# Evacuating the first two gates and values for 384 tokens early, with a transfer moved ahead and a set of copies moved later, in a fused attention and SwiGLU kernel

## Chip, cores and metric

One core of a Trainium2 chip. The metric is device time in microseconds (us), the median of several executions; the record puts all runs quoted in the fast state. Engines: PE is TensorE (matmul), PEld its weight loads, DVE is VectorE, ACT is ScalarE, POOL is GpSimd, which here issues the DMAs of the inputs and weights.

## The reference

```python
# q, k, v: (8, 8, 576, 64) = batch, head, token, dim; window 128, ALiBi slopes
scores = scale * q @ k.T                 # scale = 1/8
mask = (rel >= 0) & (rel < 128)          # rel = query position - key position
attn = softmax(where(mask, scores - slope[h] * |rel|, -1e9))
x = (attn @ v), heads joined             # (4608, 512)
g = x @ w_gate                           # (512, 1536)
out = (g * sigmoid(g) * (x @ w_val)) @ w_out     # (4608, 512) float32
```

## The kernel before

The attention works in tiles ("units") of 128 tokens; the feed-forward part works in blocks n of 512 tokens, that is four units, and in 12 column blocks m of 128. PE does every matrix product and, early on, the transposes; it writes them to PSUM, where each gate or value product fills one bank. While attention is still producing tokens, gate and value products of finished blocks fill PE. A gate is `tt` = tanh of half the product on ACT, `uu` = (tt + 1) times the product on DVE; a value product is multiplied into `hT` on DVE.

The first four units are put in order by hand. The gate and value products of m = 0, 1, 2 of block 0 are begun there for the units that are ready (`begin`), and finished when the fourth unit has been transposed:

```python
    def wide(n, m, which, c1=512):          # the product, columns c0..c1 of one PSUM bank
        ...
        for kb in range(NKB):
            nc.tensor.matmul(ps[:, c0:c1], w[:, kb, ms], xT[n][:, kb, c0:c1],
                             start=(kb == 0 and c0 == 0), stop=(kb == NKB - 1 and c1 == 512))
        if c1 < 512:
            early[(n, m, which)] = (ps, c1)
        return ps

    def gate_val(n, m):
        if n not in hT:
            hT[n] = hpool.tile([P, NMB, 512], FP16, name="hT", tag="hT")
        pg = wide(n, m, "g")
        tt = supool.tile([P, 512], FP16, name="tt", tag="tt")
        nc.scalar.activation(tt, pg, AF.Tanh, scale=0.5)
        uu = supool.tile([P, 512], FP16, name="uu", tag="uu")
        nc.vector.scalar_tensor_tensor(out=uu, in0=tt, scalar=..., in1=pg,
                                       op0=ALU.add, op1=ALU.mult)
        yield
        pv = wide(n, m, "v")
        nc.vector.tensor_mul(hT[n][:, m, :], uu, pv)
        yield

    def first_tiles():
        ...
        begin(6, 2)
        begin(4, 3)                 # g and v of m = 0, 1 for 384 tokens
        x_transposed(FIRST - 1)     # the fourth unit
        begin(6, 3)
```

The first eight steps of the feed-forward part are still in program order; after that the framework's scheduler chooses the order on PE, DVE and ACT from the dependencies:

```python
        with tc.manual_schedule(engines=ENGINES[MANUAL]):   # PE, DVE, ACT in program order
            first_tiles()
            done = FIRST
            steps = progress(ffn())
            while (at := next(steps)) < ALONE:              # ALONE = 8
                if at == 2.0:
                    nc.scalar.copy(idm2, idm)
                if at == 5.0:
                    make_masks()                            # 4 copies on ACT
        for step in steps:                                  # from here the scheduler orders
            ...
```

The loads stand in one queue:

```python
    load(4)
    load_qk(5, "q")
    load_w(512, 1024)        # W slices: 512 KB of w_gate, then 512 KB of w_val
    load_qk(5, "k")
    load_v(5)
    load_w(1024, 1536)
    load(6)                  # k6, q6, v6
    load(7)
    load(8)
    ...                      # then wo, the output weights, in two halves
```

## Time and profile before

| | before |
|---|---|
| time, median of 3 runs | 357.24 us (357.01 to 357.49) |
| PE busy in the profiled execution | 341.5 of 355.1 us |
| PE idle, 25 to 55 us | 2.71 us |
| largest PE waits there | 1.15 us (DVE), 0.81 us (q of unit 6 landing) |

PE is the bound, so a gain can only be a PE wait that goes away and is not given back later. The lines are in the prediction below. In timelines the columns are start (us), length (us), engine, source line, operation, output<-inputs, shapes, type, count; in brackets the engine's idle time just before and what ended it. "pg" and "pv" are gate and value products, "pt" transposed q or k, "ps" and "psc" scores, "px" a transposed x, "po" the output projection.

### The profile page before, as it was taken

How to read it: one execution, taken by the hardware profiler on the slowest of the kernel's cores; microseconds unless marked ns; L12 is line 12 of the kernel's file. 1: busy time of each engine (PE TensorE's matmuls, PEld its weight loads, DVE VectorE, ACT ScalarE, POOL GpSimd, SP SyncE). 2: the span in 40 equal slices, each digit the busy share in tenths (PEclk: the TensorE clock that was granted, in tenths of full speed). 3: DMA queues.
4: the chain of work that ended last, by engine and by line, in shares of the span. 5: the costliest groups of instructions: out<-in, count | busy, mean ns of one | idle time of the engine just before them, and what ended most of it. 6: DMA issues, size and time to landing. Idle time of an engine off the chain costs nothing.

```text
span 355.1 us, 7251 instructions
## 1 busy us (share of the span) xinstructions
PE 341.5 (96%) x2765; PEld 196.8 (55%) x2765; DVE 273.1 (77%) x595; ACT 178.2 (50%) x353; POOL 106.9 (30%) x132
## 2 busy tenths in 40 slices
PE   7898999999999999999999999999999999999995
PEld 4683454544456655565456655564666566456643
DVE  4858786997977799678986998799878965975540
ACT  4847584555555454555555555455444323332321
POOL 8964755544838354543500100000000000000000
PEclk9999999999999999999999999999999999999999
DMA  9999999999999999999995413311022101101114
GB/s 150 171 186 188 136 184 153 92 149 129 154 134 178 155 147 170 169 144 166 181 73 105 66 55 30 90 31 59 17 75 55 50 2 59 62 0 62 39 43 96
DMA packets 157763, 37.34 MB, mean 105 GB/s; under 512 B 147232, under 2 KB 153248, under 8 KB 157728
## 3 DMA queue, kind: packets, MB, share of 16 engines
q0 software_dynamic: 116224, 18.62, 84.3%
q1 hardware_dynamic: 41056, 17.97, 27.5%
q8 instruction: 21, 0.34, 0.4%
q10 hardware_dynamic: 448, 0.30, 0.3%
q14 instruction: 14, 0.11, 0.1%
HBM read 37.91 MB, written 9.44 MB: 133 GB/s over the span
## 4 chain that ended last, share of the span: by engine, by line
PE 71%; DVE 11%; DMA 6%; ACT 5%; POOL 4%; issue 3%; DVEq 0%; ACTq 0%; POOLq 0%
PE pg L368 21%; PE pv L368 21%; PE po L477 14%; PE av L319 4%; DMA qn<-in_q_dram 4%; PE po L398 3%; PE ps L254 3%; DVE uu L381 2%; DVE hT L385 2%; PE p L477 2%; DMA wv_sb<-in_moe_w_val_dram 2%; ACT ex L259 2%; PE px L345 2%; DVE ex L263 2%; ACT exc L286 1%
## 5 line engine op out<-in xcount | busy, mean ns | idle before, releaser
L368 PE MATMUL pg<-xT,wg_sb 128*128 128x512 f16 (+2 forms) x464 | 116.4, 365 | 0.3 <-ACT xT L346 0.2
L368 PE MATMUL pv<-xT,wv_sb 128*128 128x512 f16 (+2 forms) x464 | 114.7, 365 | 1.6 <-DVE uu L381 1.6
L379 ACT ACTIVATE tt<-pg 128x512 f16<-128x512 f32 x108 | 65.1, 604 | 85.7 <-PE pg L368 82.3
L381 DVE SCALAR_TENSOR_TENSOR uu<-tt,pg 128x512 f16<-128x512 f16 x107 | 73.0, 683 | 38.1 <-ACT tt L379 37.7
L385 DVE TENSOR_TENSOR hT<-uu,pv 128x512 f16<-128x512 f16 x108 | 73.7, 682 | 6.1 <-PE pv L368 2.3
L368 PEld LDWEIGHTS <-wv_sb 128*128 128x128 f16 x464 | 42.7, 98 | 38.8 <-issue 3.1
L368 PEld LDWEIGHTS <-wg_sb 128*128 128x128 f16 x464 | 42.4, 98 | 35.1 <-issue 2.9
L259 ACT ACTIVATE ex<-ps 128x512 f16<-128x512 f32 x96 | 50.1, 605 | 9.8 <-PE ps L254 9.8
L168 POOL DMA_DIRECT2D va<-in_v_dram x40 | 34.1, 856 | 50.3 <-PE av L319 36.0
L174 POOL DMA_DIRECT2D qn<-in_q_dram x39 | 33.6, 864 | 27.9 <-DMA qT<-qn 19.6
L174 POOL DMA_DIRECT2D kn<-in_k_dram x39 | 33.2, 860 | 25.6 <-DMA kT<-kn 15.7
L477 PEld LDWEIGHTS <-hT 128*128 128x128 f16 x336 | 31.8, 98 | 15.4 <-issue 3.5
L263 DVE TENSOR_TENSOR ex<-ex,m_reg 128x1024 f16<-128x1024 f16 x48 | 32.5, 686 | 8.3 <-ACT ex L259 8.3
L477 PEld LDWEIGHTS <-S 128*128 128x128 f16 x252 | 23.9, 98 | 11.7 <-issue 2.9
L322 DVE TENSOR_TENSOR x<-av,rec 128x256 f16<-128x256 f32 x72 | 28.9, 419 | 0.6
L477 PE MATMUL po<-T,S 128*128 128x256 f16 x168 | 23.0, 273 | 0.6 <-ACT p5s L495 0.6
L477 PE MATMUL po<-T,hT 128*128 128x256 f16 x168 | 23.1, 272 | 0.4
L286 ACT ACTIVATE exc<-psc 128x512 f16<-128x512 f32 x40 | 21.4, 608 | 3.4 <-PE psc L282 3.4
L346 ACT COPY xT<-px 128x512 f16<-128x512 f16 x24 | 14.1, 586 | 15.3 <-PE px L345 15.3
L319 PEld LDWEIGHTS <-ex 128*128 128x128 f16 x384 | 18.4, 97 | 4.9 <-issue 0.7
L319 PE MATMUL av<-va,ex 128*128 128x65 f16 x384 | 20.4, 193 | 0.5
L398 PE MATMUL po<-wo_sb,hT 128*128 128x512 f16 x84 | 19.7, 379 | 0.0
(74 smaller groups left out, 289.7 us busy)
## 6 DMA issues: line engine op xcount, KB each, us to landing
out_dram<-osb SPq DMA_DIRECT2D x32, 256.0 KB, 2.5
va<-in_v_dram POOLq DMA_DIRECT2D x32, 128.0 KB, 8.6
qn<-in_q_dram POOLq DMA_DIRECT2D x31, 128.0 KB, 8.7
kn<-in_k_dram POOLq DMA_DIRECT2D x31, 128.0 KB, 8.1
wo_sb<-in_moe_w_out_dram POOLq DMA_DIRECT2D x2, 768.0 KB, 9.4
wg_sb<-in_moe_w_gate_dram POOLq DMA_DIRECT2D x2, 512.0 KB, 10.7
wv_sb<-in_moe_w_val_dram POOLq DMA_DIRECT2D x2, 512.0 KB, 11.8
out_dram<-osb SPq DMA_DIRECT2D x6, 128.0 KB, 2.4
```

What stands on the lines that cost most here:

```text
L168: nc.gpsimd.dma_start(va[rank][p0:p1, :, 0:D], src)
L174: nc.gpsimd.dma_start(t_[p0:p1], src)
L259: nc.scalar.activation(e[:, o:o + 2, :], banks[q4][par], AF.Exp, scale=scale)
L263: nc.vector.tensor_mul(e[:, o, :], e[:, o, :], reg[:, o, :])
L319: nc.tensor.matmul(av[:, j, :], w, val, start=(n == 0), stop=(n == len(todo) - 1))
L322: nc.vector.tensor_mul(x[:, 4 * half:4 * half + 4, :], av[:, :, 0:D], rec.broadcast_to([P, 4, D]))
L368: nc.tensor.matmul(ps[:, c0:c1], w[:, kb, ms], xT[n][:, kb, c0:c1], start=(kb == 0 and c0 == 0), stop=(kb == NKB - 1 and c1 == 512))
L379: nc.scalar.activation(tt, pg, AF.Tanh, scale=0.5)
L381: nc.vector.scalar_tensor_tensor(out=uu, in0=tt, scalar=one if (n, m) == PIN else 1.0, in1=pg, op0=ALU.add, op1=ALU.mult)
L385: nc.vector.tensor_mul(hT[n][:, m, :], uu, pv)
L398: nc.tensor.matmul(po, hT[n][:, m, j * P:(j + 1) * P], wo_sb[:, m, :], start=(i == 0), stop=(i == NMB - 1))
L477: nc.tensor.matmul(dst, a[:, m, cols], b[:, m, :], start=(start and m == 0), stop=(m == HM - 1), skip_group_check=True)
```

## The change

Its intent: let ACT and DVE work off three quarters of the first two gates and values while the fourth unit is still on its way (DVE is idle there), so that DVE comes sooner to the `uu` that PE waits for; load k and q of unit 6 before v5 and the last W slices, so that PE need not wait for q6; and move the mask copies out of ACT's way to step 18.

```diff
--- before.py
+++ after.py
@@ -18,6 +18,7 @@
 WIN = 128
 QK_DMA_FROM = 11
 X_DMA_FROM = 24
+MASKS_AT = 18.0
 ALONE = 8
 MANUAL = "compute"
 ET = mybir.EngineType
@@ -366,23 +367,34 @@
             ps = pool.tile([P, 512], FP32, name="p" + which, tag=tag)
         for kb in range(NKB):
             nc.tensor.matmul(ps[:, c0:c1], w[:, kb, ms], xT[n][:, kb, c0:c1],
-                             start=(kb == 0 and c0 == 0), stop=(kb == NKB - 1 and c1 == 512))
+                             start=(kb == 0 and c0 == 0), stop=(kb == NKB - 1 and c1 == 512),
+                             skip_group_check=(n == 0))
         if c1 < 512:
             early[(n, m, which)] = (ps, c1)
         return ps
 
-    def gate_val(n, m):
+    acted = {}
+
+    def gate(n, m, pg, c0=0, c1=512):
+
+        if (n, m) not in acted:
+            acted[(n, m)] = [supool.tile([P, 512], FP16, name=i, tag=i) for i in ("tt", "uu")]
+        tt, uu = (t_[:, c0:c1] for t_ in acted[(n, m)])
+        nc.scalar.activation(tt, pg[:, c0:c1], AF.Tanh, scale=0.5)
+        nc.vector.scalar_tensor_tensor(out=uu, in0=tt, scalar=one if (n, m) == PIN else 1.0,
+                                       in1=pg[:, c0:c1], op0=ALU.add, op1=ALU.mult)
+
+    def val(n, m, pv, c0=0, c1=512):
+
         if n not in hT:
             hT[n] = hpool.tile([P, NMB, 512], FP16, name="hT", tag="hT")
-        pg = wide(n, m, "g")
-        tt = supool.tile([P, 512], FP16, name="tt", tag="tt")
-        nc.scalar.activation(tt, pg, AF.Tanh, scale=0.5)
-        uu = supool.tile([P, 512], FP16, name="uu", tag="uu")
-        nc.vector.scalar_tensor_tensor(out=uu, in0=tt, scalar=one if (n, m) == PIN else 1.0, in1=pg,
-                                       op0=ALU.add, op1=ALU.mult)
-        yield
-        pv = wide(n, m, "v")
-        nc.vector.tensor_mul(hT[n][:, m, :], uu, pv)
+        nc.vector.tensor_mul(hT[n][:, m, c0:c1], acted[(n, m)][1][:, c0:c1], pv[:, c0:c1])
+
+    def gate_val(n, m):
+        c0 = 384 if (n, m) in acted else 0
+        gate(n, m, wide(n, m, "g"), c0)
+        yield
+        val(n, m, wide(n, m, "v"), c0)
         yield
 
     def rows_of(n, j):
@@ -594,7 +606,11 @@
                 x_transposed(i - 1)
         begin(6, 2)
         begin(4, 3)
+        gate(0, 0, early[(0, 0, "g")][0], 0, 384)
         x_transposed(FIRST - 1)
+        val(0, 0, early[(0, 0, "v")][0], 0, 384)
+        gate(0, 1, early[(0, 1, "g")][0], 0, 384)
+        val(0, 1, early[(0, 1, "v")][0], 0, 384)
         begin(6, 3)
 
     def attention():
@@ -636,9 +652,10 @@
     load_qk(5, "q")
     load_w(512, 1024)
     load_qk(5, "k")
+    load_qk(6)
     load_v(5)
     load_w(1024, 1536)
-    load(6)
+    load_v(6)
     load(7)
     load(8)
     loaded = 9
@@ -675,9 +692,9 @@
             while (at := next(steps)) < ALONE:
                 if at == 2.0:
                     nc.scalar.copy(idm2, idm)
-                if at == 5.0:
-                    make_masks()
         for step in steps:
+            if step == MASKS_AT:
+                make_masks()
 
             b1 = 24 + 3 * PRE
```

`skip_group_check` only turns off a check in the framework; the refactoring into `gate` and `val` issues the same instructions where nothing is split.

> **What bounds the kernel now.** I read the page first, then the windows (busy time of each engine in chosen stretches), then the instruction timeline of the stretch the change touches, then the chain that ended last.
>
> ```profile
> PE 341.5 (96%) x2765; PEld 196.8 (55%) x2765; DVE 273.1 (77%) x595; ACT 178.2 (50%) x353; POOL 106.9 (30%) x132
> DMA  9999999999999999999995413311022101101114
> ```
>
> TensorE (PE) is busy 341.5 of 355.1 us, so at most 13.6 us can be gained by closing gaps anywhere; the DMA engines are full up to slice 22, so in the part I look at a transfer lands when its turn comes. The windows say where the gaps are. Columns: stretch, its length, busy time of PE, PEld, DVE, ACT, POOL, then clock, DMA share, GB/s.
>
> ```profile
> 20.00:30.00 10.00, 8.41 (x112) 6.59 (x109) 5.75 (x13) 6.24 (x13) 5.86 (x7) 1.00 1.72 186
> 30.00:35.00 5.00, 5.00 (x28) 2.10 (x27) 3.98 (x7) 3.04 (x6) 2.46 (x4) 1.00 1.42 197
> 35.00:40.00 5.00, 4.01 (x30) 1.89 (x29) 3.31 (x6) 2.39 (x5) 3.20 (x5) 1.00 2.46 154
> 40.00:45.00 5.00, 5.00 (x42) 2.55 (x42) 4.79 (x11) 3.62 (x7) 4.26 (x6) 1.00 1.59 128
> 45.00:50.00 5.00, 4.84 (x59) 2.61 (x57) 4.55 (x11) 4.36 (x10) 3.74 (x5) 1.00 1.21 192
> 50.00:55.00 5.00, 4.80 (x69) 2.85 (x69) 4.28 (x12) 4.49 (x10) 2.10 (x3) 1.00 2.02 167
> 200.00:250.00 50.00, 49.76 (x387) 28.27 (x386) 44.83 (x101) 25.44 (x51) 0.88 (x1) 1.00 0.22 53
> ```
>
> From about 40 us on PE is at 96 to 100%, so what PE saves before 40 us should reach the end, unless something before about 60 us gives it back. Between 20 and 40 us PE stands still for 1.59 + 0.99 = 2.6 us. The timeline names those gaps (in brackets: idle time before, and who ended it):
>
> ```profile
> 24.16 0.38 PE L368 MATMUL pg<-xT,wg_sb 128*128 128x128 f16 x4 [0.23 <-ACT xT L346]
> 27.34 0.38 PE L201 MATMUL pt<-idm,qn 128*128 128x128 f16 x4 [0.21 <-DVE uu L381]
> 28.87 1.04 PE L368 MATMUL pv<-xT,wv_sb 128*128 128x512 f16 x4 [1.15 <-DVE uu L381]
> 35.28 1.02 PE L368 MATMUL pv<-xT,wv_sb 128*128 128x512 f16 x4 [0.18 <-DVE uu L381]
> 37.34 0.40 PE L201 MATMUL pt<-idm,qn 128*128 128x128 f16 x4 [0.81 <-DMA qn<-in_q_dram]
> ```
>
> 0.23 + 0.21 + 1.15 + 0.18 + 0.81 = 2.58 us: all of it. The gap at 28.87 is the value of column block m=3, which needs the PSUM buffer that uu of m=2 reads out of. DVE comes to that one late:
>
> ```profile
> 25.21 0.69 DVE L381 SCALAR_TENSOR_TENSOR uu<-tt,pg 128x512 f16<-128x512 f16 x1 [4.07 <-ACT tt L379]
> 26.01 0.69 DVE L385 TENSOR_TENSOR hT<-uu,pv 128x512 f16<-128x512 f16 x1
> 26.23 0.63 ACT L109 COPY m_c<-m_reg 128x512 f16<-128x512 f16 x1
> 28.14 0.68 DVE L381 SCALAR_TENSOR_TENSOR uu<-tt,pg 128x512 f16<-128x512 f16 x1
> 28.53 0.60 ACT L379 ACTIVATE tt<-pg 128x512 f16<-128x512 f32 x1
> ```
>
> DVE was idle 4.07 us waiting for the first tanh, then had two full gate/value pairs to do before the uu that PE wanted; and the four mask copies (26.23 to 28.50 on ACT) held the fourth tanh until 28.53. The gap at 37.34 is tile 6's q, which the chain of waits follows back to its issue:
>
> ```profile
> 24.32 12.98 DMA qn<-in_q_dram
> 37.34 0.40 PE pt L201 x4
> ```
>
> **What the Trainium skill says.** (1) "PSUM — Partial Sum Buffer", section "PSUM bank collisions raise a hardware error": two engines may not touch one bank in the same quadrant at once, whatever the columns, so same-bank accesses of different engines are ordered by dependencies. That is the change's hidden cost: DVE reads columns 0 to 384 of a bank into which PE must still write 384 to 512. The trace before agrees: X and Y in the second product are two halves of one bank, and PE's next product into X waits for ACT's read of Y.
>
> ```profile
> 120.49 0.41 ACT L495 ACTIVATE p5s<-po 128x256 f32<-128x256 f32 x1
> 120.95 0.82 PE L477 MATMUL po<-T,S 128*128 128x256 f16 x6 [0.31 <-ACT p5s L495]
> ```
>
> (2) "ScalarE: Activation LUTs", section "What ACT_TABLE_LOAD costs": an activation with immediate scale and bias takes 186 ns + 0.833 ns per column, 613 ns for 512; the trace has 604. So splitting one in two costs one fixed part. (3) "DMA: Bandwidth & Descriptors", section "Two DMAs through the same engine are not ordered": within one queue of one engine descriptors start in order. So q of tile 6 lands behind everything issued before it; the trace agrees in size: 12.98 us to landing with two W slices ahead, 8.7 us for the median q load.
>
> **The change, part by part.** *Split gates.* Durations: tanh 604 ns for 512 columns and 290 ns for the 128-column copy of the identity on ACT, so 0.82 ns a column: 384 columns about 500 ns, 128 about 290. DVE 683 ns for 512 and 419 for 256 (row L322), so 1.03 ns a column: 550 and 290. A gate/value pair on DVE repeats every 1.40 us now (25.21 to 26.61); scaled by columns, 1.14 us for 384 and 0.61 for 128. Two more tanh and four more DVE operations cost about 0.4 us of ACT and 0.6 us of DVE in all, most of it in idle time.
>
> Laid on the trace: pg of m=0 for three tiles is ready at 22.6, tanh to 23.1 (before the xT copy at 23.52, so that copy is not delayed), uu to 23.7, hT to 24.35. The tanh of m=1 must follow the xT copy (its end 24.11): to 24.6, uu to 25.2, hT to 25.85. Now the bank rule: PE's last-tile matmuls for pg0 are free at 24.16 as today, pv0 at 24.4, but pg1 waits for uu (25.2, today 24.60) and pv1 for hT (25.9, today 24.83). So PE runs 1.05 us later here: pg2, pv2, pg3 follow to 27.4, then the three transposes (today at 26.36, 26.75, 27.34; 0.22 each) to 28.1. DVE meanwhile does the four 128-column remainders, 25.85 to 27.1, then uu of m=2 at 27.15 to 27.83 instead of 28.14 to 28.82. So pv3 starts at about 28.1 instead of 28.87: **gain 0.8 us**, not the whole 1.36, because about one microsecond of wait moves to pg1 and pv1.
>
> *Tile 6 ahead of the last W slices.* q6 jumps two W slices of 512 KB and v5 of 128 KB. At the 186 GB/s of the window 20 to 30 that is 1.15 MB / 186 = 6.2 us, so it lands at about 31 instead of 37.3. The wait of 0.81 goes, and the wait that the 0.8 us of the first part would only have lengthened does not form: **gain 0.8 us**. The W slices land later by k6 and q6, 256 KB, 1.4 us: wv landed just before 35.70 (a POOL load waited for it until then), so 37.1. Its first use is the value of m=8, at 41.07 today and about 39.4 after: still in time by 2 us.
>
> *Masks.* 2.46 us of ACT leave 26 to 28.5, where after the split the fourth tanh is wanted at 27.6; they come back after step 18, about 40 us. There ACT is busy 3.62 + 4.36 + 4.49 = 12.47 of 15 us; with 2.46 more it is 14.9 of 15. Exp, kT and xT copies queue behind the masks. PE has other matmuls to put between, and ACT is slack from 55 us (57.09 follows 1.77 us of idleness), so I charge **0.5 us**, chosen between 0 and 1.
>
> The 0.18 at 35.28 may go or stay: 0.1. wo lands at about 52.5 and is first used at 54.62; PE arrives up to 1.7 us earlier, still just behind. Sum: 0.8 + 0.8 + 0.1 - 0.5 = 1.2 us; 357.24 - 1.2 = 356.0. I shade it to **355.8**, since the fixed mask time may be hidden entirely.
>
> **The rivals.** *A, the bank wait takes it all:* if ACT starts the first tanh after the xT copy, everything of the split slides 0.6 to 1 us and PE waits on DVE in new places for as long as it does now. For it: PE is in program order here. Against: 0.4 us of margin between 23.1 and 23.52. Time: 356.3 with the load order still gaining, 357 with the mask cost. *B, ACT becomes the bound from 40 to 55 us:* 14.9 of 15 us busy; PSUM buffers come free late and PE gains holes of 1 to 2 us. Time: 357 to 357.8. *C, all 2.6 us of gaps close and the masks are free:* 354.7. *D, reshuffling:* after the first eight steps the framework's scheduler orders the instructions, and any earlier change can give another order of transposes, scores and gates over 300 us; PE's idle time there is 13.6 - 2.6 - about 4 at the start, 7 us, so I give it +-0.8 either way.
>
> **Range and chances.** The best case is near 354.5 (C with some luck of D), the poor case near 357.3 (B). Range 354.4 to 357.2. Faster by over 2% would need 7.1 us, almost three times all gaps in the stretch: 0.01. Slower by over 2%: nothing moved is that large, 0.005. Within 2%: 0.985.
>
> **What would show it right or wrong.** Right: uu and hT on 384 columns between 23 and 26 us, DVE's idle 4.07 us cut to about 2; new short PE waits "<-DVE uu" or "<-DVE hT" before the 128-column pg/pv of m=1, around 1 us in sum; pv3 near 28.1; no DMA wait before q6's transpose; PE idle in 20 to 40 us down from 2.6 to about 1.1; ACT near 100% in a stretch after 40 us with mask copies in it. Wrong: no waits at pg1 and pv1 (then bank order cost nothing and the gain is nearer 2 us); wv's last slice awaited by PE at m=8; PE holes in 40 to 55 us larger than 1 us with ACT as releaser; or a different total from gaps after 60 us, which none of my steps covers except D.

## The result

| | before | after |
|---|---|---|
| median | 357.24 us (3 runs) | 356.09 us (4 runs, 356.04 to 356.26) |
| ratio, 95% interval | | 0.9969 (0.9951 to 0.9986) |
| PE idle, 25 to 55 us | 2.71 us | 1.94 us |
| marker (below) | 32.73 us | 31.73 us |

Ratios here and below are the mean time of one kernel's fast runs over that of the other's of the same rounds, so not quite the ratio of the medians quoted. (The record of the result lists a fourth run of the kernel before, equal to the median.) The time fell by 1.15 us, which is within 2%, and inside the predicted range, 0.3 us above the predicted 355.8.

Where it came from is read in the windows of the kernel after (columns as in the prediction):

```profile
20.00:30.00 10.00, 9.12 (x117) 7.14 (x113) 6.53 (x17) 4.92 (x12) 5.80 (x8) 1.00 1.82 181
30.00:35.00 5.00, 4.72 (x32) 2.17 (x30) 3.91 (x8) 3.25 (x7) 3.27 (x6) 1.00 1.44 200
35.00:40.00 5.00, 5.00 (x42) 2.64 (x41) 4.58 (x9) 3.80 (x8) 2.59 (x4) 1.00 2.19 163
50.00:55.00 5.00, 4.26 (x54) 2.47 (x53) 4.67 (x12) 4.01 (x8) 1.75 (x2) 1.00 1.95 166
```

The first PE number is the one to follow. In 20 to 40 us PE is idle 0.88 + 0.28 + 0 = 1.16 us, where it was 2.58: the predicted 1.1. But in 50 to 55 us it is idle 0.74 us, where it was 0.20: something was given back. The PE timeline of the kernel after has both, the repaired places and the new waits:

```profile
25.34 0.38 PE L369 MATMUL pg<-xT,wg_sb 128*128 128x128 f16 x4 [0.33 <-DVE uu L384]
26.00 0.38 PE L369 MATMUL pv<-xT,wv_sb 128*128 128x128 f16 x4 [0.28 <-DVE hT L391]
...
27.75 0.22 PE L202 MATMUL pt<-idm,qn 128*128 128x128 f16 x1
28.02 1.02 PE L369 MATMUL pv<-xT,wv_sb 128*128 128x512 f16 x4
...
29.74 0.55 PE L202 MATMUL pt<-idm,qn 128*128 128x128 f16 x7
...
31.88 0.61 PE L255 MATMUL ps<-qT,kT 64*128 64x256 f16 x8
...
34.75 1.02 PE L369 MATMUL pv<-xT,wv_sb 128*128 128x512 f16 x4 [0.21 <-DVE uu L384]
...
35.83 0.39 PE L202 MATMUL pt<-idm,qn 128*128 128x128 f16 x4
...
44.00 0.61 PE L255 MATMUL ps<-qT,kT 64*128 64x256 f16 x8
...
51.32 0.29 PE L346 MATMUL px<-idm,x 128*128 128x128 f16 x2 [0.23 <-DVE x L323]
...
52.25 0.28 PE L346 MATMUL px<-idm,x 128*128 128x128 f16 x2 [0.32 <-DVE x L323]
...
56.09 0.81 PE L410 MATMUL po<-wo_sb,hT 128*128 128x512 f16 x3
```

The bank waits are there (0.33 and 0.28), pv of m = 3 starts at 28.02 without a wait, and q6 is transposed at 35.83 without one. The wait of 0.21 us for `uu` at 34.75 stayed, and two new waits for `x` of the attention stand at 51.32 and 52.25. The last lines answer to these of the kernel before, its PE timeline:

```profile
29.84 0.28 PE L254 MATMUL ps<-qT,kT 64*128 64x256 f16 x2
...
44.81 0.62 PE L254 MATMUL ps<-qT,kT 64*128 64x256 f16 x8
...
56.89 0.81 PE L398 MATMUL po<-wo_sb,hT 128*128 128x512 f16 x3
```

The first scores after the hand-ordered part start at 29.84 before and at 31.88 after, which is taken up with the experiments. The scores that start at 44.81 start 0.81 us earlier after the change, and the last three matmuls of the first output projection, at 56.89, start 0.80 us earlier.

On DVE the idle 4.07 us ahead of the first `uu` are halved, and its 384 columns take the predicted 0.55 us (DVE timeline of the kernel after):

```profile
23.36 0.55 DVE L384 SCALAR_TENSOR_TENSOR uu<-tt,pg 128x384 f16<-128x384 f16 x1 [2.00 <-ACT tt L383]
```

The mask copies, moved to step 18 in the text, were to appear on ACT after 40 us. ACT's timeline has the first of them here:

```profile
7.04 0.62 ACT L110 COPY m_c<-m_reg 128x512 f16<-128x512 f16 x1
```

All four run from 7.04 to 9.31 us, right after the exponentials that make their source. The scheduler, free to place them, put them *earlier*, into time when ACT had been idle waiting for the first scores (2.14 us before the change, 0.20 now). "Later" in the program was 19 us earlier on the chip.

**A marker.** The start of a run jitters: the last-unit matmuls of pg0 start at 24.16 in the profiled execution of the kernel before, at 24.36 after, and between 23.8 and 24.8 in the experiments, in no relation to their edits. Absolute times of different traces therefore carry some 0.5 us of noise. (PE's wait for q6 in the kernels with the old load order is the exception: it ends between 37.32 and 37.67 in all five traces.) I take as marker the time from those matmuls (the line at 24.16 in the prediction) to the last three matmuls of the first output projection (56.89 and 56.09): 56.89 - 24.16 = 32.73 before, 56.09 - 24.36 = 31.73 after. It fell by 1.0 us, the time by 1.15. In all fourteen traces the stretch from the first to the last of these holds the same 276 matmuls, kind by kind, so that the marker compares equal work in different orders. After about 57 us PE's idle time agrees between the kernels, stretch by stretch (0.27 us in 60 to 80, 0.46 in 80 to 100, 0.98 in 150 to 200, 0.24 in 200 to 250), so nearly all of the difference arises inside the marker.

### The profile page after: what moved, and what is told of

It is laid out like the page before. It is cut to its first block, busy times and chain, and to the rows that moved or that the text cites. A ratio compares the mean times of both kernels' runs of the same rounds, so it can differ in the third digit from the quotient of the medians.

```text
span 354.5 us, 7261 instructions
## 1 busy us (share of the span) xinstructions
PE 341.5 (96%) x2765; PEld 197.5 (56%) x2765; DVE 273.4 (77%) x599; ACT 178.9 (50%) x355; POOL 106.9 (30%) x132
## 2 busy tenths in 40 slices
DMA packets 157763, 37.34 MB, mean 105 GB/s; under 512 B 147232, under 2 KB 153248, under 8 KB 157728
## 4 chain that ended last, share of the span: by engine, by line
PE 73%; DVE 16%; ACT 7%; issue 3%; DVEq 0%; ACTq 0%
PE pv L369 20%; PE pg L369 20%; PE po L489 14%; PE av L320 4%; DVE uu L384 4%; DVE hT L391 3%; PE ps L255 3%; PE po L410 3%; DVE ex L264 3%; PE p L489 2%; ACT ex L260 2%; PE px L346 2%; ACT tt L383 2%; ACT exc L287 2%; DVE x L323 1%
## 5 line engine op out<-in xcount | busy, mean ns | idle before, releaser
L383 ACT ACTIVATE tt<-pg 128x512 f16<-128x512 f32 (+2 forms) x110 | 65.5, 596 | 85.2 <-PE pg L369 81.8
L384 DVE SCALAR_TENSOR_TENSOR uu<-tt,pg 128x512 f16<-128x512 f16 (+2 forms) x109 | 73.4, 674 | 34.6 <-ACT tt L383 33.9
L391 DVE TENSOR_TENSOR hT<-uu,pv 128x512 f16<-128x512 f16 (+2 forms) x110 | 74.0, 673 | 7.1 <-PE pv L369 2.2
L347 ACT COPY xT<-px 128x512 f16<-128x512 f16 x24 | 14.1, 586 | 14.9 <-PE px L346 14.8
```

The lines of the kernel that those rows point to most:

```text
L383: nc.scalar.activation(tt, pg[:, c0:c1], AF.Tanh, scale=0.5)
L384: nc.vector.scalar_tensor_tensor(out=uu, in0=tt, scalar=one if (n, m) == PIN else 1.0, in1=pg[:, c0:c1], op0=ALU.add, op1=ALU.mult)
L391: nc.vector.tensor_mul(hT[n][:, m, c0:c1], acted[(n, m)][1][:, c0:c1], pv[:, c0:c1])
```

## The experiments

**Theory.** The load order gives the whole gain. The split does locally what was worked out, but alters the order that the scheduler gives PE afterwards, and what it wins is lost through that order. **Rivals:** (1) the bank waits take the split's gain; (2) each part gives its predicted share (0.8, 0.8, -0.5); (3) the masks cost time where they are.

The experiments ran in three groups of four, each with its own runs of the kernel before beside it (medians 357.06 to 357.20), each group on another chip (7, 10 and 2 in the record), so that kernels of different groups are compared by their ratios to before. All had 5 rounds, and all gave the right result. PE idle is over 25 to 55 us of the profiled execution; it is a coarser measure than the marker, as its edges don't move with the jitter.

| kernel | median us (range) | ratio to before (95%) | marker | PE idle |
|---|---|---|---|---|
| before | 357.24 | 1 | 32.73 | 2.71 |
| the change | 356.09 | 0.9969 (0.9951 to 0.9986) | 31.73 | 1.94 |
| e_split_only | 358.27 (358.19 to 358.45) | 1.0033 (1.0020 to 1.0045) | 33.90 | 3.71 |
| e_load_only | 355.92 (355.61 to 356.30) | 0.9968 (0.9955 to 0.9980) | 31.75 | 1.90 |
| e_masks_only | 356.99 (356.78 to 357.18) | 0.9996 (0.9983 to 1.0010) | 32.38 | 2.35 |
| e_load_masks | 356.18 (355.96 to 356.43) | 0.9973 (0.9961 to 0.9986) | 31.75 | 1.90 |
| e_split_load | 357.06 (356.86 to 358.78) | 1.0003 (0.9988 to 1.0018) | 32.79 | 2.82 |
| e_split_masks | 357.78 (357.68 to 358.05) | 1.0017 (1.0005 to 1.0029) | 33.11 | 3.12 |
| e_masks_late | 355.85 (355.80 to 356.29) | 0.9963 (0.9951 to 0.9976) | 31.70 | 1.83 |
| e_fill | 354.94 (354.77 to 356.16) | 0.9942 (0.9930 to 0.9954) | 30.43 | 0.85 |
| e_qk_first | 355.81 (354.84 to 357.82) | 0.9963 (0.9941 to 0.9986) | 30.55 | 1.00 |
| e_one_early | 355.27 (354.91 to 357.69) | 0.9961 (0.9939 to 0.9984) | 30.59 | 1.10 |
| e_fill_masks_old | 355.69 (354.85 to 358.13) | 0.9964 (0.9940 to 0.9988) | 32.07 | 2.43 |
| e_fill_old_load | 358.61 (356.84 to 358.91) | 1.0025 (1.0007 to 1.0043) | 34.00 | 2.61 |

### The three parts, alone

**Only the split.** The load order and the place of the masks are those of before:

```diff
--- the change
+++ e_split_only
-    load_qk(6)
     load_v(5)
     load_w(1024, 1536)
-    load_v(6)
+    load(6)
@@
                     nc.scalar.copy(idm2, idm)
+                if at == 5.0:
+                    make_masks()
         for step in steps:
-            if step == MASKS_AT:
-                make_masks()
```

> The kernel before with the split gates alone (old load order, masks still made at step 5). Theory A (the parts hang on one another): q of tile 6 lands near 37.3 us whatever PE does before it, so all that the split wins by 28 us is lost again in a longer wait before q6's transpose: wait there 0.8 -> about 1.3 to 1.6 us, total 357.0 to 357.3, same as before. Rival B (the parts add up): the split gives 0.5 us or more by itself, total at or below 356.7, wait at q6 no longer.

Measured: 358.27 us, slower than before, ratio 1.0033 with an interval above 1; marker 33.90, 1.2 us longer. That is 1 us above even the 357.0 to 357.3 expected. PE's timeline:

```profile
30.70 1.02 PE L369 MATMUL pv<-xT,wv_sb 128*128 128x512 f16 x4 [0.51 <-DVE uu L384]
...
37.35 0.40 PE L202 MATMUL pt<-idm,qn 128*128 128x128 f16 x4 [1.24 <-DMA qn<-in_q_dram]
...
53.71 0.28 PE L346 MATMUL px<-idm,x 128*128 128x128 f16 x2 [0.66 <-DVE x L323]
```

Two things are to be seen. The wait for q6 has grown from 0.81 to 1.24 us and ends at 37.35, as it did before (37.34): the landing does not move with PE, and what PE wins ahead of it is spent waiting at it. All of the loss therefore comes after it, where there are waits for the attention's `x` (0.66 us at 53.71) that the kernel before did not have. Rival 2 does not hold: the split alone is worth less than nothing.

**Only the load order.** The split's four calls are taken out and the masks are at step 5 again:

```diff
--- before
+++ e_load_only
+    load_qk(6)
     load_v(5)
     load_w(1024, 1536)
-    load(6)
+    load_v(6)
```

> The kernel before with the load order alone. Theory A: q6 lands near 31 us, the 0.81 us wait before its transpose goes, the 1.15 us gap at 28.87 stays; PE ahead by 0.8 us at 40 us and, since the stretch up to 57 us gives nothing back as long as no more than about 0.8 is won, total 356.4 to 356.6. Rival C (the attention chain from 42 to 54 us sets the time whatever is won before it): no change, 357.1 to 357.3.

Measured: 355.92 us, ratio 0.9968, marker 31.75. The change as a whole has 0.9969 and 31.73. PE's timeline:

```profile
28.56 1.04 PE L369 MATMUL pv<-xT,wv_sb 128*128 128x512 f16 x4 [1.15 <-DVE uu L384]
...
36.05 0.39 PE L202 MATMUL pt<-idm,qn 128*128 128x128 f16 x4
```

The wait of 1.15 us for `uu` is untouched, the wait for q6 is gone. It is faster than either reading expected. Two lines of edit give as much as the whole change.

**Only the masks.**

```diff
--- before
+++ e_masks_only
                     nc.scalar.copy(idm2, idm)
-                if at == 5.0:
-                    make_masks()
         for step in steps:
+            if step == MASKS_AT:
+                make_masks()
```

> The kernel before with the masks alone moved to step 18. The built order puts the four mask copies right after the eight exponentials of the first masks, near 7 us, not later: ACT waits there for the first scores anyway. Theory A: fourth tanh comes earlier, but PE then waits the longer for q6 (37.3): 357.0 to 357.3. Rival B (parts add): 0.2 to 0.4 us gained, 356.9. A third reading: the copies at 7 us delay the first exp by 0.2 us (the kernel after starts its first exp 0.2 us later than before), then 357.4; if the first exp starts at 9.3 with the masks in front, that 0.2 was chance.

Measured: 356.99 us, ratio 0.9996 (0.9983 to 1.0010): no difference that the runs can tell. The marker is 0.35 us shorter only because this trace starts 0.33 us late (24.49) while the wait for q6 ends where it did (37.32): where PE waits for a landing, the jitter of the start enters the marker.

### The three parts, in pairs

**Without the split:** the change with these four lines taken out.

```diff
--- the change
+++ e_load_masks
-        gate(0, 0, early[(0, 0, "g")][0], 0, 384)
         x_transposed(FIRST - 1)
-        val(0, 0, early[(0, 0, "v")][0], 0, 384)
-        gate(0, 1, early[(0, 1, "g")][0], 0, 384)
-        val(0, 1, early[(0, 1, "v")][0], 0, 384)
         begin(6, 3)
```

> The change without the split gates (load order and masks). Theory A: the 1.15 us gap at 28.87 stays near 1 us since it hangs on DVE's order, the q6 wait goes; total 356.3 to 356.6, so the split's share on top is 0.2 to 0.5 us. Rival C: what is won before 42 us beyond about 0.8 us is taken back by the attention chain, so this is already as fast as the whole change, 356.1.

Measured: 356.18 us, ratio 0.9973, marker 31.75. Its interval and that of the change overlap almost wholly: **inside the change the split is worth nothing that the runs can tell**, where 0.8 us had been predicted.

**Without moving the masks:** the change with `make_masks()` back at step 5 (the mask lines of the first diff above).

> The change without the move of the masks (made at step 5, on ACT near 26 to 29 us). Theory A with free masks: the mask copies hold the fourth tanh back to about 28.5 us and the uu of m=3 to about 29.5; PE has other work, so 0 to 0.3 us slower than the change: 356.1 to 356.4. If the masks were the larger part of what was won: 356.7 or more.

Measured: 357.06 us, ratio 1.0003 (five of six runs 356.86 to 357.23, one 358.78), marker 32.79. The split and the load order together, with masks in their old place, gain nothing. `make_masks` at step 5 puts 2.3 us of copies on ACT just before the tanh of m = 3; PE then waits at 30.81 for the `uu` that follows:

```profile
30.81 1.02 PE L369 MATMUL pv<-xT,wv_sb 128*128 128x512 f16 x4 [0.51 <-DVE uu L384]
```

In the trace DVE itself had been idle 1.31 us for that tanh. After this wait PE's order is another one than in the change. So beside the split the old place of the masks costs about 1 us; how much of it is this wait and how much the order, these runs don't separate. Rival 3 is partly right: the masks matter, but only together with the split.

**Without the load order:** the change with `load(6)` behind the W slices again (the load lines of the first diff above).

> The change without the load order. Theory A: PE is at q6's transpose about 1.5 us early and waits about 1.5 to 2.2 us for it; total 357.0 to 357.3, the same as before. Rival B: 356.5, as the split keeps its own share.

Measured: 357.78 us, ratio 1.0017, marker 33.11. PE waits 1.21 us for q6, to 37.63. This is slower than before, by more than the expectation had it (357.0 to 357.3), and the wait is shorter than the 1.5 us or more expected. Beside the change (0.9969) the load order is worth 0.0048, 1.7 us: more than alone. Without it the wait there is 0.4 us longer than before (1.21 against 0.81).

### Where the split's gain went

**Masks really late.** As the scheduler had hoisted the copies, the cost that I had charged them had not been tried. Here they are held behind the tanh of m = 8:

```diff
--- the change
+++ e_masks_late
+    tanhs = []
@@
-        nc.scalar.activation(tt, pg[:, c0:c1], AF.Tanh, scale=0.5)
+        tanhs.append(nc.scalar.activation(tt, pg[:, c0:c1], AF.Tanh, scale=0.5))
@@
             if step == MASKS_AT:
-                make_masks()
+                with tc.issue_after(tanhs[-1].ins):
+                    make_masks()
```

> The change with the four mask copies forced behind the tanh of m=8 on ACT (near 40 us), which is what the prediction took the change to do. The prediction's step: ACT then close to full from 40 to 55 us and 0.5 us (0 to 1) lost against the change: 356.6. Rival: PE has enough other work, or the scheduler orders around it: 356.1, no difference.

Measured: 355.85 us, ratio 0.9963, marker 31.70: no slower than with the masks at 7 us. The copies start at 40.22 in its trace. The predicted cost of 0.5 us does not come even where the copies are as late as I had assumed.

**The bank waits filled.** The change finishes m = 1 before it takes up m = 2. Here PE does the last-unit matmuls of m = 2, whose banks nobody is reading, before those of m = 1, while DVE reads the banks of m = 1:

```diff
--- the change
+++ e_fill
+    whole = {}
@@
-        gate(n, m, wide(n, m, "g"), c0)
+        gate(n, m, whole.pop((n, m, "g"), None) or wide(n, m, "g"), c0)
         yield
-        val(n, m, wide(n, m, "v"), c0)
+        val(n, m, whole.pop((n, m, "v"), None) or wide(n, m, "v"), c0)
+        if (n, m) == (0, 0):
+            for which in "gv":
+                whole[(0, 2, which)] = wide(0, 2, which)
         yield
```

> The change with the last-tile matmuls of m=2 issued on PE before those of m=1, so that PE has 0.45 us of work while DVE still reads the two banks of m=1. Theory: the waits of 0.33 and 0.28 us before pg1 and pv1 come from the reads of the first 384 columns in the same bank; they shrink by about 0.45 us in sum. In the total: 355.7 if what is won there reaches the end; 356.1 (no change) if, as theory C has it, the attention chain between 42 and 54 us takes back whatever is won before it.

Measured: 354.94 us, ratio 0.9942 (0.9930 to 0.9954), marker 30.43. It beats both kernels, and its interval just does not meet that of e_load_only (on another chip): here the split does gain, and more than the 355.7 expected at best. The marker is 1.3 us shorter than the change's, though, and the bank waits had only 0.33 + 0.28 = 0.61 us to give (one of them, 0.28, remains). The rest must come from elsewhere. The order on PE shows what: in the kernel before PE does the transposes k4, q4, q5 (12 matmuls) and then pv of m = 3. In the change it does k4, one matmul of q4 (27.75 in the fence of the result), pv of m = 3, the next gate, and only then the other seven (29.74). So the scores that need q5 (keys of unit 4, queries of units 4 and 5; the recorded expectation below calls them those of unit 5) start 7.5 us after the marker's start instead of 5.7. In e_fill the order is the old one, and those scores start at 5.7 again. Filling the waits and the order are mixed in this experiment; the next takes them apart.

**The order restored, the bank waits kept.** The transposes of unit 4 are put into the hand-ordered part, ahead of pv of m = 3; nothing else changes:

```diff
--- the change
+++ e_qk_first
                     nc.scalar.copy(idm2, idm)
+                if at == 7.0:
+                    transposes_to(need[FIRST])
         for step in steps:
```

> The change with the transposes of k4, q4 and q5 put by hand before pv3 (in the kernel after, the scheduler does only one of q4's, then pv3 and pg4, then the other seven, so that the first scores of unit 5 start 7.5 us after the last-tile pg0 instead of 5.7 as before; from there on all of PE's order differs from before). The bank waits before pg1 and pv1 stay (0.6 us). Theory D (the split earns nothing in the change because of that other order): from the transposes on the order is that of before, scores at about 6 us, the lead of PE kept up to the end of block 0, total 355.2 to 355.7. Rival (the bank waits themselves eat the gain): 356.0 to 356.2 as the change.

Measured: median 355.81 us, ratio 0.9963, in neither of the two ranges expected. The profiled execution took 354.98 us, with marker 30.55 and PE idle 1.00 us. The timeline of PE:

```profile
25.35 0.38 PE L369 MATMUL pg<-xT,wg_sb 128*128 128x128 f16 x4 [0.33 <-DVE uu L384]
26.01 0.38 PE L369 MATMUL pv<-xT,wv_sb 128*128 128x128 f16 x4 [0.28 <-DVE hT L391]
...
27.76 0.61 PE L202 MATMUL pt<-idm,qn 128*128 128x128 f16 x8
...
30.08 0.61 PE L255 MATMUL ps<-qT,kT 64*128 64x256 f16 x8
...
54.92 0.81 PE L410 MATMUL po<-wo_sb,hT 128*128 128x512 f16 x3
```

All eight matmuls of q4 and q5 stand together, and the scores follow at 30.08. The bank waits are still 0.33 and 0.28 us, the same as in the change, and yet the marker is 1.2 us shorter than the change's (31.73) and than that of e_load_only (31.75). **Rival 1 falls:** the bank waits do not take the split's gain. The order did: with it kept, the split is worth 31.75 - 30.55 = 1.2 us in the marker, somewhat more than predicted. Why the scheduler chose the other order, no run shows.

How an order costs PE time is read from the traces and not tested by itself. The matmuls are the same. Gates that PE takes before the scores are gates that it no longer has to put into the pauses of the attention chain (scores, exp, multiplication, weighted values, x), and those pauses then show as waits for `x`: 0.23 us at 51.32 and 0.32 at 52.25 in the change; neither e_load_only nor e_qk_first has them (each is idle 0.20 us in 50 to 55, the change 0.74). The times of this kernel have two values, three of six near 355.0, the others 356.3 to 357.8, so its ratio of 0.9963 does not separate it from the change; the argument rests on the markers, one trace of each kernel, and the 1.2 us is what the better half of the runs shows. More on this below.

**Only the first gate and value early.**

```diff
--- the change
+++ e_one_early
         val(0, 0, early[(0, 0, "v")][0], 0, 384)
-        gate(0, 1, early[(0, 1, "g")][0], 0, 384)
-        val(0, 1, early[(0, 1, "v")][0], 0, 384)
         begin(6, 3)
```

> The change with only the first gate and value evacuated early, not the second: no wait before pg1 and pv1, DVE has one full pair (1.40 us) and one 128-column pair (0.61) to do before the uu of m=2; the built order is like before after the transposes. If the early second gate is worth its bank waits: 355.7 to 356.0; if the first gate alone brings it: 355.0 to 355.4, near the fill version's 354.95.

Measured: 355.27 us, ratio 0.9961, marker 30.59. The bank waits are gone, and pv of m = 3 waits 0.61 us for `uu` instead: as much as the two together (0.61). The order is the good one. So the second early gate and value only move a wait from one place to another, and half of the split does as well as all of it. With the new load order, the four kernels with a split and the old order of transposes have markers of 30.43 to 30.59 (after a wait for `wo` in one of them, below, is taken off), the three with the other order 31.70 to 32.79: the order goes with the gain in all seven.

### What comes next on the path

**Filled, with the masks in the old place:** e_fill with `make_masks()` at step 5.

> The fill version with the masks back at step 5 (26 to 29 us on ACT); its PE order is the same as the fill version's, so this is the cost of the masks by themselves. Theory: the fourth tanh waits for the four copies (about 2 us later), PE waits 0.5 us for a uu: 355.4 to 355.6 against 354.95. Rival (masks only mattered through the order they caused, 1.1 us between the change and the change without the move): no difference, 354.9 to 355.1.

Measured: 355.69 us, ratio 0.9964; three of its six runs lie at 354.9 to 355.2, the others above 356. Up to the output projection, 28.1 us after the marker's start, PE's timeline is that of e_fill to within 0.1 us, but for one matmul that changes sides of the first scores, and the wait of 0.5 us expected for `uu` is not there: with that order of PE, the old place of the masks costs nothing. But the profiled execution (356.19 us) has a wait that e_fill's (354.82 us) has not, here at PE and at POOL:

```profile
53.92 1.89 PE L414 MATMUL po<-wo_sb,hT 128*128 128x512 f16 x8 [1.64 <-DVE x L323]
```

```profile
54.16 1.75 POOL L169 DMA_DIRECT2D va<-in_v_dram  x2 [4.59 <-DMA wo_sb<-in_moe_w_out_dram]
```

The profile names DVE's `x`, but DVE had long finished it; POOL's next load, which waited for `wo`, the output weights, until 54.16, shows what landed then. Without the 1.64 us the marker is 32.07 - 1.64 = 30.43, e_fill's to the digit. POOL's wait for `wo` ends between 52.27 and 53.37 in the other thirteen traces, and e_fill starts the projection at 52.50. So in the kernels that are fast up to there PE arrives just when the second half of `wo` lands, and a late landing costs it a wait. In this run that accounts for the 1.4 us beside e_fill's; that the other runs above 356 us wait there too is likely, but no profile caught one. The runs at 357.7 to 358.1 in this group (and the 358.78 of e_split_load) remain unexplained, but the record has a hint: their mean granted clock is 0.994 or 0.995, while no other run of the kernels named so far is below 0.997.

**Filled, with the old load order:** e_fill with `load(6)` behind the W slices.

> The fill version with the old load order, PE order again the same. Theory A: PE is at q6's transpose about 2.1 us before it lands (37.3 us) and waits for it: all that is won before is lost, total 356.9 to 357.2, like the kernel before. Rival: part is kept, 356.0 or less.

Measured: 358.61 us, ratio 1.0025: slower than before, and than the 356.9 to 357.2 expected, though it is the best kernel but for two lines. PE's timeline, and its windows around that place:

```profile
37.67 0.40 PE L202 MATMUL pt<-idm,qn 128*128 128x128 f16 x4 [1.96 <-DMA qn<-in_q_dram]
```

```profile
36.00:37.00 1.00, 0.00 (x0) 0.00 (x0) 0.59 (x1) 0.34 (x1) 0.75 (x2) 1.00 2.43 155
38.60:39.60 1.00, 1.00 (x4) 0.30 (x2) 0.00 (x0) 0.06 (x1) 0.41 (x1) 0.50 2.26 144
```

The wait for q6 has grown to 1.96 us, and the column after POOL's, the granted clock, drops from 1.00 to 0.50 right after it (0.81 on the average of 37.6 to 38.6, 0.50 to 41.6, then back to 1.00). At half clock for some 3 us PE loses about 1.5 us more, an estimate from these windows; the marker agrees, as it is 34.00 - 30.43 = 3.57 us longer than e_fill's, 1.96 of it the wait. Waits of 1.21 and 1.24 us at the same place (e_split_masks, e_split_only) left the clock at 1.00, and so did the 1.64 us ahead of the output projection in e_fill_masks_old. The times of this kernel are 356.84 and 357.25 in two runs and 358.46 to 358.91 in four, which would fit a drop that comes in most runs. Their mean clocks are 0.993 to 0.997, most of them below every run of the kernel before, but that of 356.84 is 0.995 as well, and only one run was profiled. By the ratios to before, as the two ran on different chips, the load order is worth 1.0025 - 0.9942 = 0.0083, 3.0 us, beside the filled split (about half of it the lost clock, by the estimate above), and 1.15 us without the split.

## Why the prediction was right in the sum and wrong in two of its steps

- **Total.** Predicted 355.8, measured 356.09. The sum was right by luck, as errors cancelled: the split was credited 0.8 us that did not arrive and the 0.1 us for the wait at 35.28 did not come, while the masks were charged 0.5 us that did not fall due and the load order gave some 0.35 us more than its 0.8.
- **"Tile 6 ahead ... gain 0.8 us":** right in mechanism, and the size was a little small: 1.0 us in the marker and 0.0032 of 357, 1.15 us, in time, by e_load_only. The wait at q6 is gone, and the last W slice landed by 37.42, when a POOL load stopped waiting for it; predicted 37.1. PE never waited for it. (That q6 lands behind all that was issued before it is more than "start in order" says; in the trace before it did so, 37.3 against 35.7 us for the last W slice.)
- **"Split gates ... gain 0.8 us":** the local working held almost to the tenth. DVE's idle time fell to 2.00 us (predicted about 2), pg1 came at 25.34 (25.2), pv1 at 26.00 (25.9), pv of m = 3 at 28.02 (28.1). What failed was the sentence that what PE saves before 40 us "should reach the end, unless something before about 60 us gives it back". Something did: the order of PE's work behind the first gates, with pv of m = 3 and a gate put ahead of seven of the eight transposes of q4 and q5. I had that as rival D and gave it +-0.8; it took all of the gain, as e_load_masks shows (0 with the order of the change: markers 31.75 and 31.73) against e_qk_first (1.2 us of marker with the old order).
- **"Masks ... I charge 0.5 us":** wrong. The copies did not come after 40 us but at 7 us, since nothing held them there, and e_masks_late, which does hold them back, costs nothing either (0.9963 against 0.9969). ACT was busy 13.2 us of the 15 from 40 to 55 us there, not 14.9. ACT's summed busy time in 40 to 55 us was no measure of what PE would wait: PE had other matmuls.
- **"The 0.18 at 35.28 may go or stay":** it stayed, 0.21 us at 34.75.
- **Rival A**, the bank waits take it all: the waits came, 0.61 us in sum (I had said around 1), but pv of m = 3 started as early as worked out, and e_qk_first keeps them and gains. **Rival B**, ACT the bound: no run shows it, and e_masks_late, which puts the copies there, speaks against it. **Rival C**, all gaps close and the masks are free, 354.7: the change does not get there; e_fill, which closes most, has 354.94.

What would have helped to see it: the prediction followed three waits by name and took the matmuls behind them as fixed in order. A look at which side of the hand-ordered section each moved instruction falls on would have shown that the masks were free to go anywhere.

## What to carry to other kernels

A transfer that lands at a fixed time swallows whatever is won ahead of it, so move the transfer first and then shorten what comes before; here the two lines of load order gained 1.15 us alone and were worth 3.0 us beside the best version of the split, in part because the longer wait was followed by a lower clock. Where a scheduler orders part of the kernel, a small gain can change the order behind it by more than its own size, and an instruction moved down in the text can run earlier: compare the order of instructions of two traces before their durations, and pin the order that the gain needs. Half of an early evacuation can be worth as much as all of it when the other half only moves a wait onto a bank that is being read.

## What the Trainium skill lacked or had wrong

- "PSUM — Partial Sum Buffer", section "PSUM bank collisions raise a hardware error": nothing lacking; the page has it that different addresses of one bank still collide, and the trace agrees. PE's last-unit matmuls into columns 384 to 512 waited 0.33 us (pg1) and 0.28 us (pv1) for DVE's reads of columns 0 to 384 of the same banks, and do not wait in e_one_early, where DVE does not read these banks early.
- "TensorE: Matmul & The Clock Gate", section "HAM oscillation — how this bites in real kernels", puts the rule as "no PE-idle gaps >~3.4µs". In e_fill_old_load a wait of 1.96 us was followed by a granted clock of 0.50 for some 3 us. The page's half clock agrees; as a rule of thumb for safe gaps 3.4 us is too long in this one trace. Waits of 1.21, 1.24 and 1.64 us left the clock at 1.00; between 1.64 and 1.96 us no run here tells.
- No page has it: that an instruction moved later in the program of a scheduled region can run earlier on the chip (the mask copies, 26.2 us before, 7.0 us after), and that the order of PE's work alone, with the same waits on banks, can be worth 1.2 us (the change against e_qk_first, marker 31.73 and 30.55).
- No page has it: that the profile's named releaser can be one that was long done. The 1.64 us ahead of the output projection in e_fill_masks_old is put down to DVE, while the POOL queue shows the output weights landing at that time.
